# Two pairs of heads of every tile from 4 to 10 turned by way of DRAM, in a fused attention and mixture-of-experts kernel on one core

## Chip, core and metric

The kernel runs on one core of a Trainium2 chip, as one launch. The metric is the device time in microseconds (us) from the start to the end of a launch. Before the change the median of three runs is 717.74 us (717.74 to 717.99).

## What is computed

A banded attention feeds four weighted experts, whose output feeds a gated layer with a norm. All tensors are float32.

```python
def _attn_ref(q, k, v, n_global, n_local):          # 2 x 8 heads x 768 x 64, 8 global and 96 local keys
    ...
    scores = scale * np.matmul(q, k.transpose(0, 1, 3, 2))
    ...
    keep = is_global | is_local
    scores = scores + bias[None, :, :, :]           # a slope per head times the distance
    scores = np.where(keep, scores, -1000000000.0)
    a = np.exp(scores - np.max(scores, axis=-1, keepdims=True))
    a = a / (np.sum(a, axis=-1, keepdims=True) + 1e-09)
    return np.matmul(a, v).astype(np.float32)

def _moe_ref(x, domain_probs, w1, w2):              # 1536 tokens, 512 -> 1024 -> 512, 4 experts
    p = domain_probs / (domain_probs.sum(-1, keepdims=True) + 1e-09)
    for e in range(E):
        h = np.maximum(x @ w1[e], 0.0)
        out += p[:, e:e + 1] * (h @ w2[e])
    return out.astype(np.float32)

def _moe2_ref(x, w_in, w_out, g_ln):                # 512 -> 1024 -> 512
    h = x @ w_in
    e = np.exp(h - h_max)
    sm = e / (np.sum(e, axis=-1, keepdims=True) + 1e-09)
    solu = h * sm
    ln = (solu - mu) / np.sqrt(var + 1e-06) * g_ln
    return (ln @ w_out).astype(np.float32)
```

## The kernel before

The 1,536 tokens are 12 tiles of 128, and a tile's 8 heads are 4 pairs. A unit u is one pair of heads of one tile, tile u // 4 and pair u % 4, so there are 48 units. From unit 14 on the loop at lines 1578 to 1640 takes two units at a time: iteration t forms the scores of units t and t + 1, and brings earlier units further. The scheduler keeps the written order on each engine; an engine takes its instructions one after the other.

For a unit the steps are these. `scores` (L1224): TensorE forms sps, of which there is one buffer with room for two units, so the scores of t + 2 wait until VectorE has read those of t. `soft_pair` first sums and inverts the row sums of the units before (su, L1261 and L1262) and scales their probabilities p (L1266, on VectorE or GpSimd), then VectorE adds the bias and finds the row minimum (L1275, a custom instruction for each head, four per iteration), and ScalarE takes the exponential (L1282). Then p must be transposed, as TensorE needs the keys on the partitions. `stage_b` does it on TensorE (tile pt, L1306) and ScalarE copies the result out (pts, L1308). For the first two pairs of the tiles in `TURNED` the way is another: `turn` has VectorE transpose 32 x 32 blocks (L1324) and writes them to DRAM (t_dram, L1326), and two iterations later `turned_back` reads them into the one tile pts_turned with four transfers that put the blocks in place (L1331). In both ways `stage_c` multiplies by the values (x, L1357); a tile that is complete is rounded to xh on ScalarE (L1370) and its remainder xl is formed on VectorE (L1371), which is the input of the experts.

Between these steps TensorE is filled with products of the experts. They come from one generator in a fixed order, expert half 0 over the token blocks of 256, 256, 512 and 512 columns. `pull(share)` takes products until their cost has used up the credit, where `share` grows by what the iteration has not to do itself (`other`). A block can begin only when `tokens[0]` has reached its end: the third block needs 1,024 tokens, tiles 0 to 7. `tokens[0]` is set from `done` in the second half of an iteration. In a block's first GEMM (L553, from xh and xl) the fourth group's result fhh is made on VectorE (L565) and its remainder fhl too (L568); the second GEMM (L584) reads both, and VectorE weights its result into scr (L589).

GpSimd scales p, copies the overlap of the key tiles (L95) and, from t = 36 (`FORMS`), forms sums of xh and xl (L801) that begin with tiles 0 to 7. SyncE's queue issues every transfer of this stretch: values v (L1198), the write to t_dram, keys kr (L93), queries q (L1193) and the four reads.

```python
other = 870 * (not turned(t - 2)) + 550 * len(valued(t)) + 1100 * turned(t - 8)
share = 2 * (EARLY if t < N0 + 27 else LATE) + (1970 - other) // 2
```

Of the kernel before, what the change touches and what calls it, by code (L numbers as in the profile page):

```python
# [44 lines left out]
LOAD_AFTER = {2: [4], 3: [5], 4: [6], 5: [7], 6: [8, 9], 7: [10], 8: [11]}  # L45
SHARE = {11: 1000}
HALF = 512
PAIRS = 14
FORMS = 36
TURNED = 4, 6, 8, 9, 10  # L50
# [4 lines left out]
def kernel(ctx, tc, ep, qk, vp, nn, pr, wall, w64, gl, out):  # L55
# [1093 lines left out]
    def fast_arm():  # L1149
        st = stream("f")  # L1150
        with ExitStack() as es:
# [104 lines left out]
            def soft_pair(t):  # L1256

                if PAIRS < t <= NU:
                    st_rs.pop(t - 2), st_rs.pop(t - 1)
                    su = ss.tile([128, 4], F32, tag="su2", name="su2")  # L1260
                    nc.vector.tensor_reduce(out=su, in_=sums[:, (t // 2 - 1) % 3], op=ALU.add, axis=AX.X)  # L1261
                    nc.vector.reciprocal(out=su, in_=su)  # L1262
                    for u in (t - 2, t - 1):
                        p = st_p[u]
                        e = nc.gpsimd if turned(u) or t < NU and (u % 2 or t > FORMS) else nc.vector
                        e.tensor_tensor(out=p, in0=p, in1=su[:, 2 * (u % 2):2 * (u % 2) + 2].unsqueeze(2)  # L1266
                                        .to_broadcast([128, 2, 256]), op=ALU.mult)
# [43 lines left out]
            def turned(u):  # L1311

                return u % 4 < 2 and u // 4 in TURNED

            def valued(t):

                if turned(t - 4) or turned(t - 8) and t <= NU:
                    return []
                return list(range(t - 6 if turned(t - 10) and not turned(t - 6) else t - 4, t - 2))

            def turn(u0):
# [4 lines left out]
                nc.sync.dma_start(out=t_dram[u0 // 4 % 2], in_=blocks)  # L1326

            def turned_back(u0):
                t = pts_turned
                for jj in range(4):  # L1330
                    nc.sync.dma_start(out=t[32 * jj:32 * jj + 32].rearrange("r (i c) -> r i c", i=4),  # L1331
                                      in_=t_dram[u0 // 4 % 2].rearrange("(i r) (j c) -> j r i c", r=32, j=4)[jj])
# [4 lines left out]
            def stage_c(u, hold=None):  # L1337
# [23 lines left out]
                elif u >= N0 and pr_ == (1 if turned(u) else 3) and not turned(u - 2):  # L1361
# [216 lines left out]
            for t in range(PAIRS, NU + 3, 2):  # L1578

                other = 870 * (not turned(t - 2)) + 550 * len(valued(t)) + 1100 * turned(t - 8)  # L1580
# [6 lines left out]
                if turned(t - 8) and t <= NU:  # L1587
# [7 lines left out]
                if turned(t - 8):  # L1595
# [15 lines left out]
                for _ in range(2):  # L1611
                    next(rest_p, None)
                if t <= NU and not turned(t - 2):
# [12 lines left out]
                if t > NU and turned(t - 6):  # L1626
                    pull(share)
                    for u in (t - 6, t - 5):
                        stage_c(u)
# [3 lines left out]
                elif turned(t - 8):  # L1633
# [191 lines left out]
```

## Time and profile before

| | us |
|---|---|
| median of three runs (lowest, highest) | 717.74 (717.74, 717.99) |
| the profiled execution, its own time | 718.38 |
| its span in the trace | 716.6 |
| TensorE busy in it | 706.1 |
| VectorE, ScalarE, GpSimd busy | 497.8, 302.1, 349.2 |

The profile is of one execution. Its span is the time from the first to the last instruction, 1.8 us less than the execution's time. A line of a timeline gives the start in the span, the duration, the engine, the line of the kernel, what is written from what, how often in a row, and, in brackets, idle time before it with what ended it. Matmuls overlap, so what one costs is read from the start of one to the start of the next.

### The profile page before, as it was taken

What the parts mean: (1) busy time and instruction counts of PE and PEld (TensorE: products, weight loads), DVE (VectorE), ACT (ScalarE), POOL (GpSimd) and SP (SyncE); (2) the same over time, 40 slices, a digit from 0 to 9 for tenths busy, and PEclk for the clock granted to TensorE, in tenths of its full rate; (3) what the DMA queues carried; (4) which work ended last, traced back from release to release, by engine and by line L of the source; (5) the groups of instructions that cost most, each with busy time, mean ns of one, the idle gap of its engine ahead of it and who ended that gap; (6) DMA issues with size and microseconds to landing.
All of it is one profiled execution on the core that took longest, in us unless ns stands there. A gap on an engine that the chain in (4) does not pass through costs nothing.

```text
span 716.6 us, 11078 instructions
## 1 busy us (share of the span) xinstructions
PE 706.1 (99%) x3823; PEld 587.7 (82%) x3823; DVE 497.8 (69%) x1086; ACT 302.1 (42%) x678; POOL 349.2 (49%) x407
## 2 busy tenths in 40 slices
PE   7999999999999999999999999999999999999997
PEld 5688778888888889888888988888898888888886
DVE  6777665648776675776668578857964677777870
ACT  5877655432423333242243334324334324454442
POOL 6733475674883074227307323630745189455500
PEclk9999999999999999999999999999999999999999
DMA  8656762321351323233133323323322680424331
GB/s 251 153 162 167 181 172 88 102 74 45 111 164 49 118 91 101 82 95 118 45 117 113 95 73 118 118 77 100 103 89 74 267 349 1 137 101 138 106 124 49
DMA packets 59201, 84.56 MB, mean 118 GB/s; under 512 B 6144, under 2 KB 36608, under 8 KB 59136
## 3 DMA queue, kind: packets, MB, share of 16 engines
q1 hardware_dynamic: 58576, 83.34, 37.0%
q8 instruction: 32, 0.52, 0.3%
q10 hardware_dynamic: 560, 0.43, 0.2%
q14 instruction: 33, 0.27, 0.1%
HBM read 62.22 MB, written 21.52 MB: 117 GB/s over the span
## 4 chain that ended last, share of the span: by engine, by line
PE 95%; DVE 1%; ACT 1%; SPq 1%; DMA 1%; issue 0%; POOL 0%; DVEq 0%
PE fg L584 37%; PE fg L761 19%; PE fo L1089 9%; PE fh L990 8%; PE fg L676 7%; PE fg L553 6%; PE x L1357 3%; PE sps L1224 2%; PE pt L1306 2%; PE g L1384 1%; PE wp L135 1%; DMA pts_turned<-t_dram 1%; DVE fg L689 1%; ACT fhh L645 1%; PE fh L1070 0%
## 5 line engine op out<-in xcount | busy, mean ns | idle before, releaser
L584 PE MATMUL fg<-fhh,wV 128*128 128x512 f32 (+1 forms) x800 | 242.3, 384 | 0.4
L584 PEld LDWEIGHTS fg<-fhh,wV 128*128 128x128 f32 x800 | 148.0, 188 | 32.7 <-issue 2.7
L584 PE MATMUL fg<-fhl,wV 128*128 128x512 f32 (+1 forms) x400 | 149.1, 381 | 0.1
L584 PEld LDWEIGHTS fg<-fhl,wV 128*128 128x128 f32 x400 | 74.9, 188 | 14.9 <-DVE fhl L568 0.4
L310 POOL TENSOR_TENSOR wR<-kr,wR 128x512 fp32r<-128x512 f32 (+1 forms) x28 | 29.0, 1057 | 96.5 <-ACT wR L302 96.3
L645 ACT ACTIVATE fhh<-fg 128x512 fp32r<-128x512 f32 x80 | 47.5, 598 | 66.6 <-DVE fg L771 40.3
L603 POOL TENSOR_TENSOR scr<-scr,kr 128x512 f32<-128x512 f32 x24 | 31.0, 1292 | 61.4 <-DVE kr L602 61.4
L646 DVE SCALAR_TENSOR_TENSOR fhl<-fg,fhh 128x512 fp32r<-128x512 f32 x80 | 54.1, 687 | 6.9 <-ACT fhh L645 5.4
L761 PE MATMUL fg<-xt,fwS 128*128 128x512 f32 x252 | 58.3, 389 | 0.0
L761 PEld LDWEIGHTS fg<-xt,fwS 128*128 128x128 f32 x252 | 47.3, 188 | 9.8
L761 PE MATMUL fg<-xh,wR 128*128 128x512 f32 x168 | 54.0, 389 | 0.0
L771 DVE TENSOR_TENSOR fg<-kr,fg 128x512 f32<-128x512 f32 x42 | 29.1, 694 | 33.4 <-PE fg L761 22.9
L598 DVE TENSOR_TENSOR fg<-fg,pb 128x512 f32<-128x512 f32 x59 | 40.9, 693 | 15.1 <-PE fg L584 14.8
L1266 POOL TENSOR_TENSOR p<-p,su 128x512 f32<-128x512 f32 x24 | 27.9, 1178 | 38.7 <-ACT pts L1308 17.6
L1282 ACT ACTIVATE p<-p,mn 128x256 f32<-128x256 f32 x68 | 33.8, 499 | 23.3 <-DVE mn L1275 23.2
L599 DVE TENSOR_TENSOR scr<-fg,scr 128x512 f32<-128x512 f32 x59 | 40.8, 692 | 2.0
L553 PE MATMUL fg<-xh,wR 128*128 128x512 f32 (+1 forms) x128 | 38.9, 373 | 0.0
L761 PEld LDWEIGHTS fg<-xh,wR 128*128 128x128 f32 x168 | 31.5, 188 | 6.5
L310 POOL TENSOR_TENSOR fwS<-kr,fwS 128x512 fp32r<-128x512 f32 x28 | 35.7, 1296 | 1.6 <-ACT fwS L302 1.6
L1089 PE MATMUL fo<-xt,fhh 128*128 128x512 f32 (+1 forms) x156 | 35.4, 375 | 0.0
L766 ACT COPY kr<-fg 128x512 f32<-128x512 f32 x42 | 24.2, 590 | 25.6 <-PE fg L761 25.6
L1275 DVE CUSTOM_DVE_ANT_0 p<-sps,btab 128x256 f32<-128x256 f32 x68 | 25.0, 420 | 14.2 <-PE sps L1224 14.2
(286 smaller groups left out, 1503.3 us busy)
## 6 DMA issues: line engine op xcount, KB each, us to landing
w_dram<-fr SPq DMA_DIRECT2D x44, 256.0 KB, 2.4
kr<-in_wall_dram SPq DMA_DIRECT2D x42, 256.0 KB, 2.8
fr<-in_w_dram SPq DMA_DIRECT2D x32, 256.0 KB, 2.7
pb<-p_dram SPq DMA_DIRECT2D x22, 256.0 KB, 3.5
v<-in_vp_dram SPq DMA_DIRECT2D x10, 512.0 KB, 4.4
kr<-t_dram SPq DMA_DIRECT2D x32, 128.0 KB, 2.9
frawt<-in_wall_dram SPq DMA_DIRECT2D x14, 256.0 KB, 2.7
xt<-w_dram SPq DMA_DIRECT2D x6, 512.0 KB, 10.2
```

The lines of the kernel that those rows point to most:

```text
L310: e.tensor_tensor(out=w[:, 1], in0=t, in1=w[:, 0].bitcast(F32), op=ALU.subtract)
L553: nc.tensor.matmul(ps[:, :n], lhsT=w[:, a, k], rhs=b[:, k, cols], start=(k == 0 and i == 0), stop=(k == 3 and i == 2))
L584: nc.tensor.matmul(ps[:, :n], lhsT=w[:, a, k], rhs=b[k], start=(i == 0), stop=(i == 11))
L598: nc.vector.tensor_tensor(out=ps[:, :n], in0=ps[:, :n], in1=pg, op=ALU.mult)
L599: nc.vector.tensor_tensor(out=a, in0=ps[:, :n], in1=a, op=ALU.add)
L645: nc.scalar.activation(th, src, AF.Relu)
L646: residuals.append(lambda: nc.vector.scalar_tensor_tensor(out=tl, in0=src, scalar=0.0, in1=th.bitcast(F32), op0=ALU.max, op1=ALU.subtract))
L676: nc.tensor.matmul(ps[:, q_ * q:q_ * q + q_], lhsT=w[:, a, j], rhs=x[b][j], start=(opens and q == j == m == 0), stop=(j == 1 and m == 2), ...
L761: nc.tensor.matmul(ps, lhsT=w[:, a, j], rhs=x[b][j], start=(i in (1, 2, 5) and j == 0 and m == 0), stop=(j == 1 and m == 2), skip_group_ch ...
L990: nc.tensor.matmul(ps[i], lhsT=left[i][x][j], rhs=right[i][j][:, y], start=(i in (1, 5, 2) and j == m == 0), stop=(j == 1 and m == 2), ski ...
L1089: nc.tensor.matmul(ps, lhsT=a[:, fc % 4], rhs=wo[fc][:, i % 2, c0:c0 + n], start=(fc == i == 0), stop=(fc == 7 and i == 2))
L1282: nc.scalar.activation(p[:, a], p[:, a], AF.Exp, bias=mn[:, a:a + 1], scale=-1.0, accum_out=st_rs[u][:, a, 0:1])
```

## The change

Two pairs of heads, units 4s and 4s + 1, of each tile s from 4 to 10 are turned through DRAM; before, tiles 5 and 7 were transposed by TensorE. `ended(t)` says that t is the iteration in which a tile's turned units of t - 8 are valued. `BOTH`, empty here, would name tiles whose other two pairs are turned as well, and the code for it adds nothing as long as it is empty. The place in t_dram was by tile, `u0 // 4 % 2`, and is by pair now, `u0 // 2 % 2`, which is 0 for all units that are turned. The table `LOAD_AFTER` brings the keys of one tile per tile. Unit 15 is scaled on VectorE instead of GpSimd.

```diff
--- before.py
+++ after.py
@@ -42,12 +42,13 @@
 
 RING = 4
 KEY_OF = [0, NI] + list(range(1, NI)) + list(range(NI + 1, 2 * NI))
-LOAD_AFTER = {2: [4], 3: [5], 4: [6], 5: [7], 6: [8, 9], 7: [10], 8: [11]}
+LOAD_AFTER = {2: [4], 3: [5], 4: [6], 5: [7], 6: [8], 7: [9], 8: [10], 9: [11]}
 SHARE = {11: 1000}
 HALF = 512
 PAIRS = 14
 FORMS = 36
-TURNED = 4, 6, 8, 9, 10
+TURNED = 4, 5, 6, 7, 8, 9, 10
+BOTH = ()
 LATE = 680
 
 
@@ -1262,7 +1263,7 @@
                     nc.vector.reciprocal(out=su, in_=su)
                     for u in (t - 2, t - 1):
                         p = st_p[u]
-                        e = nc.gpsimd if turned(u) or t < NU and (u % 2 or t > FORMS) else nc.vector
+                        e = nc.gpsimd if turned(u) or t < NU and (u % 2 and t > PAIRS + 2 or t > FORMS) else nc.vector
                         e.tensor_tensor(out=p, in0=p, in1=su[:, 2 * (u % 2):2 * (u % 2) + 2].unsqueeze(2)
                                         .to_broadcast([128, 2, 256]), op=ALU.mult)
                 for u in (t, t + 1) if t < NU else ():
@@ -1310,26 +1311,30 @@
 
             def turned(u):
 
-                return u % 4 < 2 and u // 4 in TURNED
+                return u // 4 in (TURNED if u % 4 < 2 else BOTH)
 
             def valued(t):
 
-                if turned(t - 4) or turned(t - 8) and t <= NU:
+                if turned(t - 4) or ended(t) and t <= NU:
                     return []
-                return list(range(t - 6 if turned(t - 10) and not turned(t - 6) else t - 4, t - 2))
+                return list(range(t - 6 if t % 4 == 2 and turned(t - 10) and not turned(t - 6) else t - 4, t - 2))
+
+            def ended(t):
+
+                return t % 4 == 0 and turned(t - 8)
 
             def turn(u0):
                 for u in (u0, u0 + 1):
                     p, k = st_p.pop(u), 4 * (u % 2)
                     nc.vector.transpose(out=blocks.rearrange("p (jj c q) -> p c jj q", jj=4, c=8)[:, k:k + 4],
                                         in_=p.rearrange("p a (c jj f) -> p (a c) jj f", c=2, jj=4))
-                nc.sync.dma_start(out=t_dram[u0 // 4 % 2], in_=blocks)
+                nc.sync.dma_start(out=t_dram[u0 // 2 % 2], in_=blocks)
 
             def turned_back(u0):
-                t = pts_turned
+                t = pts_all[:, 2:4].rearrange("p u c q -> p (u c q)") if u0 % 4 else pts_turned
                 for jj in range(4):
                     nc.sync.dma_start(out=t[32 * jj:32 * jj + 32].rearrange("r (i c) -> r i c", i=4),
-                                      in_=t_dram[u0 // 4 % 2].rearrange("(i r) (j c) -> j r i c", r=32, j=4)[jj])
+                                      in_=t_dram[u0 // 2 % 2].rearrange("(i r) (j c) -> j r i c", r=32, j=4)[jj])
                 t = t.rearrange("p (i c q) -> p c i q", i=4, c=8)
                 for u in (u0, u0 + 1):
                     st_pt[u] = [t[:, 4 * (u % 2) + c] for c in range(4)]
@@ -1358,7 +1363,7 @@
                                          start=(c == 0), stop=(c == nch - 1))
                 if u < N0 and s == NAT - 1:
                     xc = slice(pr_, pr_ + 1), slice(0, 128 * NAT)
-                elif u >= N0 and pr_ == (1 if turned(u) else 3) and not turned(u - 2):
+                elif u >= N0 and pr_ == (1 if s in TURNED and s not in BOTH else 3):
                     xc = slice(0, 4), slice(128 * s, 128 * s + 128)
                 else:
                     return
@@ -1577,14 +1582,14 @@
                     st.load_piece()
             for t in range(PAIRS, NU + 3, 2):
 
-                other = 870 * (not turned(t - 2)) + 550 * len(valued(t)) + 1100 * turned(t - 8)
+                other = 870 * (not turned(t - 2)) + 550 * len(valued(t)) + 1100 * ended(t) * (1 + turned(t - 6))
                 share = 2 * (EARLY if t < N0 + 27 else LATE) + (1970 - other) // 2
                 hold, landed = [], copies[:]
                 del copies[:]
                 if t < NU:
                     for u in (t, t + 1):
                         scores(u)
-                if turned(t - 8) and t <= NU:
+                if ended(t):
                     for u in (t - 8, t - 7):
                         stage_c(u, hold)
                 if t < NU:
@@ -1592,7 +1597,7 @@
                         next_operands(*divmod(u, 4))
                 if turned(t - 4):
                     turned_back(t - 4)
-                if turned(t - 8):
+                if ended(t):
                     load_v((t - 8) // 4 + 2)
                 soft_pair(t)
                 for f in landed:
@@ -1610,6 +1615,9 @@
                     pull(share)
                 for _ in range(2):
                     next(rest_p, None)
+                if ended(t) and turned(t - 6):
+                    for u in (t - 6, t - 5):
+                        stage_c(u)
                 if t <= NU and not turned(t - 2):
                     for u in (t - 2, t - 1):
                         stage_b(u)
@@ -1623,14 +1631,10 @@
                 for u in valued(t):
                     if u in st_pt:
                         stage_c(u)
-                if t > NU and turned(t - 6):
-                    pull(share)
-                    for u in (t - 6, t - 5):
-                        stage_c(u)
                 if t % 4 == 2 and not turned(t - 6):
                     done = (t - 2) // 4
                     load_v(done + 1)
-                elif turned(t - 8):
+                elif ended(t):
                     done = (t - 4) // 4
                 if t == FORMS:
                     st.forms = st.x_forms(lambda: [st.rawp.tile([128, 512], F32, tag="raw", name="fraw")
```

On TensorE, iterations t = 34 and 36 before (a scores instruction in four parts opens each; fg is an expert's product, pt a transpose, x the values):

```order
L1224 MATMUL sps<-kr,q 128x256 x4
L584 MATMUL fg<-fhh,wV 128x256
L584 MATMUL fg<-fhl,wV 128x256
L584 MATMUL fg<-fhh,wV 128x256 x2
L584 MATMUL fg<-fhl,wV 128x256
L584 MATMUL fg<-fhh,wV 128x256
L1357 MATMUL x<-pts,v 64x128 x16
L1224 MATMUL sps<-kr,q 128x256 x4
L1306 MATMUL pt<-ident,p 128x128 x8
L553 MATMUL fg<-xh,wR 128x512
L553 MATMUL fg<-xl,wR 128x512
L553 MATMUL fg<-xh,wR 128x512 x2
L553 MATMUL fg<-xl,wR 128x512
```

The same engine now, from the scores of t = 32 to those of t = 38 and the first product behind them:

```order
L1225 MATMUL sps<-kr,q 128x256 x4
L1362 MATMUL x<-pts_turned,v 64x128 x8
L1307 MATMUL pt<-ident,p 128x128 x8
L1225 MATMUL sps<-kr,q 128x256 x4
L1362 MATMUL x<-pts,v 64x128 x8
L1225 MATMUL sps<-kr,q 128x256 x4
L1362 MATMUL x<-pts_turned,v 64x128 x8
L1307 MATMUL pt<-ident,p 128x128 x8
L1225 MATMUL sps<-kr,q 128x256 x4
L554 MATMUL fg<-xh,wR 128x512
```

The products of t = 32, 34 and 36 have moved to earlier iterations (up to t = 30) and to later ones, so scores, turned values, transposes and values follow each other.

On VectorE, from the second custom of t = 28 to the first weighting, before (the ISA rows are the customs and their minima):

```order
L1275 ISA mn 128x1
L1371 TENSOR_TENSOR xl<-x,xh 128x4x128
L1275 ISA p,mn<-sps,btab 128x256
L1275 ISA mn 128x1
L1275 ISA p,mn<-sps,btab 128x256
L1275 ISA mn 128x1
L565 TENSOR_SCALAR fhh<-fg 128x256
L568 SCALAR_TENSOR_TENSOR fhl<-fg,fhh 128x256
L589 TENSOR_TENSOR scr<-fg,pb 128x256
```

The same work now stands at t = 26, behind the turn of units 24 and 25 (tmp_170 is the block buffer):

```order
L1276 ISA p,mn<-sps,btab 128x256
L1276 ISA mn 128x1
L1329 STREAM_TRANSPOSE tmp_170<-p 128x4x4x32 x2
L566 TENSOR_SCALAR fhh<-fg 128x256
L569 SCALAR_TENSOR_TENSOR fhl<-fg,fhh 128x256
L590 TENSOR_TENSOR scr<-fg,pb 128x256
L1262 TENSOR_REDUCE su_1017<-sums 128x4
L1263 RECIPROCAL su_1017<-su_1017 128x4
```

The fourth group's fhh and fhl and the first weighting have moved from behind the customs of t = 28 to right behind the turn of t = 26.

On SyncE, from the write of t = 26 to the next reads, before:

```order
L1326 DMA t_dram<-tmp_170 128x1024
L1198 DMA v<-in_vp_dram 128x1024
L93 DMA kr<-in_qk_dram 64x4x128 x4
L1193 DMA q<-in_qk_dram 64x4x128 x2
L1331 DMA pts_turned<-t_dram 32x4x256 x4
L93 DMA kr<-in_qk_dram 64x4x128 x2
L1193 DMA q<-in_qk_dram 64x4x128 x2
```

Now:

```order
L1331 DMA t_dram<-tmp_170 128x1024
L94 DMA kr<-in_qk_dram 64x4x128 x2
L1194 DMA q<-in_qk_dram 64x4x128 x2
L1336 DMA pts_turned<-t_dram 32x4x256 x4
L1199 DMA v<-in_vp_dram 128x1024
L1331 DMA t_dram<-tmp_170 128x1024
```

The values v stand behind the reads, two key transfers instead of four ahead of them, and a turn's transfers stand in every second iteration.

## Rows read from the trace of the kernel before

**Rows 1.** The page, busy time of the engines and the chain that ended last.
```profile
PE 706.1 (99%) x3823; PEld 587.7 (82%) x3823; DVE 497.8 (69%) x1086; ACT 302.1 (42%) x678; POOL 349.2 (49%) x407
...
PE 95%; DVE 1%; ACT 1%; SPq 1%; DMA 1%; issue 0%; POOL 0%; DVEq 0%
```

**Rows 2.** The waits of TensorE from 40 to 250 us: total, times, longest.
```profile
PE x L1357 <- DMA pts_turned<-t_dram: 0.5, 1, 0.5
PE pt L1306 <- DVE p L1266: 0.3, 1, 0.3
PE pt L1306 <- POOL p L1266: 0.2, 1, 0.2
```

**Rows 3.** Timeline of TensorE from 43 to 61 us, t = 18 to 26.
```profile
43.48 0.39 PE L584 MATMUL fg<-fhh,wV 128*128 128x256 f32 x1
...
46.17 1.09 PE L1357 MATMUL x<-pts,v 128*64 128x128 f32 x16
...
52.88 0.39 PE L553 MATMUL fg<-xh,wR 128*128 128x256 f32 x1
...
53.70 1.03 PE L1306 MATMUL pt<-ident,p 128*128 128x128 f32 x8
54.49 0.36 PE L553 MATMUL fg<-xh,wR 128*128 128x256 f32 x1
...
55.38 1.09 PE L1357 MATMUL x<-pts,v 128*64 128x128 f32 x16
...
60.98 1.13 PE L1224 MATMUL sps<-kr,q 64*128 64x256 f32 x8
```

**Rows 4.** Timeline of TensorE at t = 28, from 67 to 70 us.
```profile
67.80 1.03 PE L1306 MATMUL pt<-ident,p 128*128 128x128 f32 x8
...
69.33 0.39 PE L584 MATMUL fg<-fhl,wV 128*128 128x256 f32 x1
```

**Rows 5.** Timeline of VectorE: the turn of t = 26, fhh of t = 28.
```profile
63.88 1.29 DVE L1324 STREAM_TRANSPOSE tmp<-p 128x512 f32<-128x512 f32 x2
...
68.40 0.42 DVE L565 TENSOR_SCALAR fhh<-fg 128x256 fp32r<-128x256 f32 x1
```

**Rows 6.** Timeline of GpSimd: scalings of t = 26, first sums at t = 36.
```profile
61.83 2.04 POOL L1266 TENSOR_TENSOR p<-p,su 128x512 f32<-128x512 f32 x2 [4.24 <-PE sps L1224]
...
86.78 1.29 POOL L801 TENSOR_TENSOR fraw<-xh,xl 128x512 f32<-128x512 f32 x1 [0.47 <-DVE xl L1371]
```

**Rows 7.** Timeline of TensorE at t = 32, scores and turned values.
```profile
75.06 1.14 PE L1224 MATMUL sps<-kr,q 64*128 64x256 f32 x8
76.70 1.09 PE L1357 MATMUL x<-pts_turned,v 128*64 128x128 f32 x16 [0.50 <-DMA pts_turned<-t_dram]
```

**Rows 8.** Timeline of VectorE from 76 to 85 us, t = 32 to 36.
```profile
76.25 0.42 DVE L1275 CUSTOM_DVE_ANT_0 p<-sps,btab 128x256 f32<-128x256 f32 x1 [0.87 <-PE sps L1224]
...
79.35 0.69 DVE L1371 TENSOR_TENSOR xl<-x,xh 128x512 fp32r<-128x512 f32 x1 [0.18 <-ACT xh L1370]
...
80.15 0.18 DVE L1262 RECIPROCAL su<-su 128x4 f32<-128x4 f32 x1
...
84.71 0.69 DVE L1266 TENSOR_TENSOR p<-p,su 128x512 f32<-128x512 f32 x1
```

**Rows 9.** Timeline of ScalarE at t = 32: xh, behind the exponentials.
```profile
78.76 0.56 ACT L1370 CAST xh<-x 128x512 fp32r<-128x512 f32 x1
```

**Rows 10.** SyncE's queue: the write of t = 26 and its reads.
```profile
65.20 0.34 SPq L1326 DMA_DIRECT2D t_dram<-tmp  x1
...
70.20 2.02 SPq L1331 DMA_DIRECT2D pts_turned<-t_dram  x4
```

**Rows 11.** The tile pts_turned: time from issue to landing.
```profile
DMA to landing us min/median/max: 2.5/4.3/5.5
```

**Rows 12.** Windows of core 0: busy time of engines, clock, DMA share.
```profile
0.00:20.00 20.00, 16.42 (x97) 10.72 (x97) 13.34 (x75) 11.13 (x44) 13.38 (x30) 1.00 0.83 249
...
710.00:716.60 6.60, 1.52 (x13) 1.32 (x11) 0.00 (x0) 0.47 (x1) 0.00 (x0) 0.77 0.16 50
```

## The prediction

> **What bounds the kernel now.** I read the page first: TensorE is busy 706.1 of 716.6 us and the chain of waits that ended last lies on it for 95% [rows 1]. So a change pays only if TensorE has less to do or waits less. The waits of TensorE from 40 to 250 us are three, 1.0 us together: for the DMA that brings turned probabilities back, and for two scalings of p [rows 2]. The changed stretch, iterations t = 14 to 48 of attention, has hardly anything to gain but TensorE's own work, and much that can be uncovered. Then I read the timelines of TensorE, VectorE, GpSimd and SyncE for t = 20 to 40.
>
> **What is removed.** Units 20, 21, 28 and 29 are no longer transposed by TensorE: two pairs of units, 16 transposes. At t = 22 such a pair starts at 53.70 and the next product at 54.49, so 0.79 us [rows 3]. It also cuts a run of MoE products in two. 21 products in one run take 2.69 us (43.48 to 46.17), 0.128 each; the 12 products around this pair take 52.88 to 55.38 less 0.79, 1.71, where one run would take 1.54. So 0.17 for a cut, and 0.96 for a pair: 1.9 for both. By the order of instructions the products of t = 20 to 48 stand in six runs fewer than before; two of the six are the pairs', four more at 0.17 give 0.7. Saved: **2.6 us**. ScalarE loses four copies of pts, GpSimd and VectorE exchange a few scalings; neither sets the pace there, so nothing.
>
> **What is moved: the fill.** The planner counts 870 ns less beside a turned pair, so it pulls more MoE products into t = 22 to 30. The first two blocks (256 columns) are then used up at t = 30, where before they last to t = 34. The third block needs 1,024 tokens, which stand ready once tile 7 is valued. Tile 7's end moves from t = 34 to t = 36, since its first pair now comes back through DRAM; block 3 starts at t = 38 instead of 36. So t = 32, 34 and 36 have no product at all. No product is lost: 18 of 512 columns just come after attention. This costs in three places.
>
> **Wait A, t = 26.** Before, the first products of the second GEMM stand at t = 28, behind scores and customs alone, and wait 0.6 us: the pair of transposes starts at 67.80, the second product after it at 69.33 where 68.71 would be due [rows 4]. Now nine of them come at t = 26 without waiting and the tenth needs fhh of ft 3, which VectorE makes behind the two transposes of units 24 and 25. Those wait for GpSimd's two scalings. Before, GpSimd ends them at 63.87 and VectorE turns from 63.88 for 1.29 us [rows 5, 6]. The turn that t = 22 gains puts up to 1.2 us ahead of this on VectorE, of which its idle time takes a part: I take 0.7 later. Turn done 65.3, fhh 0.4 on [rows 5], 65.7, fhl 66.0. TensorE starts these scores at 61.2 (60.98 before [rows 3], and 0.2 more as t = 22 now has 21 products and no pair), needs 1.07 for them and 12 x 0.128 for the products, and stands at 63.8. **2.2 us**; with no shift 1.5, with all of it 2.7.
>
> **Wait B, t = 32 to 38.** Without products an iteration is as long as the chain of softmax, as scores has one buffer. The steps show at t = 32 of before: scores start at 75.06, the first custom at 76.25, the four exponentials are done and xh starts at 78.76, xl at 79.35, the reciprocal of the sums ends at 80.33 [rows 7 to 9]. That is 5.27 from scores to sums, 2.51 from first custom to last exponential. Where scores(32) start follows from TensorE's own work: scores(26) at 61.2; t = 26 with 18 products, 2.3, wait A and a value of a pair, 1.0, brings scores(28) to 67.8; t = 28 with turned values, 1.0, and 12 products and a pair of transposes, 2.5, brings scores(30) to 72.4; t = 30 with 21 products, 2.7, and a value brings scores(32) to 77.1. From there the sums are ready at 82.4, the exponentials of t = 34 at 84.9, sums 0.6 later, a scaling on VectorE 0.65 [rows 8], four customs 1.4: 87.6, when scores(38) may start. TensorE's own work in between is three scores (3.2), two turned values (2.0), two pairs of transposes (1.6), one value of a pair (1.0), 7.9 of 10.5 us. So 2.6 idle. Then block 3's first product waits for xl of tile 7: exponentials of t = 36, xh 0.59, xl 0.61, at 89.85, while scores(38) end at 88.67: 1.2. **3.8 us**. Bounds: 2.6 if xl of tile 7 comes in time after all, 4.5 if transposes and values also wait for their scaling and copies in turn.
>
> **Wait C, t = 40 and 44.** From t = 36 on GpSimd has sums of x between its scalings, and they stand first in its queue. The first waits for xl of tile 7: before it starts at 86.78, and GpSimd then has two sums of 1.3 and two scalings of 2.04 by turns [rows 6]. From 89.85 two sums, p(36, 37), two sums end at 97.1, and p(38) and p(39) at 98.1 and 99.1. TensorE reaches their transposes at 96.7: from 89.85 nine products of 512 columns, each counted as two of 256 (0.24), a value, scores, turned values, and six more products. 1.4 for the one and 0.7 for the other, 2.1, and by the same count 0.7 at t = 44. That is **2.8 us**, within 0.5 (if TensorE comes later than I count) and 4.
>
> **The DRAM round trip.** A turn is now due every 4 steps, with one buffer (t_dram[0]) and one tile pts_turned; the next write waits until the last read-back has landed, the next read-back until the values of the pair before are formed. Its price: before, a write at 65.20, the first read at 70.20, and values at 76.70 that had waited for it, so 11.4 in all [rows 10, 7], with v and four key transfers ahead of the reads. Now v stands behind the reads and two key transfers are ahead; a single read lands after 2.5 to 5.5, median 4.3 [rows 11]. I take 8.6, within 7.5 and 11.4. By 8.6 the values of t = 36 come when TensorE is there, so nothing is added; at 9.8 waits of 2.0 and 2.6 at t = 36 and 40 take the place of C, and the sum grows by about 1. The Trainium skill (SBUF — State Buffer, The DMA setup-cost knee) fits a transfer as 2 us plus its bytes at 436 GB/s; for 512 KB each way that is an estimate of 3.2 + 3.2 = 6.4 us and would add nothing. The rows show nearly twice that, so I go by them.
>
> **Small parts.** Unit 15's scaling on VectorE is 0.69 [rows 8] at t = 16; no row shows TensorE waiting near it, and it delays customs by at most 0.7: 0, at worst 0.5. Keys one tile later: scores of tile 9 need them at t = 36, loaded from t = 32: more than 8 us against 3 to 5; 0. The eight reads and two writes more keep SyncE's queue waiting; behind them stand v and later keys, needed an iteration on: 0.
>
> **Sum.** New waits 2.2 + 3.8 + 2.8 = 8.8. Old waits that go: 1.0 [rows 2] and 0.6 [rows 4]. Saved work 2.6. 8.8 - 1.6 - 2.6 = **+4.6 us**. After attention TensorE has no idle time until the last microseconds, so nothing is given back. On the profiled execution (718.38 us, span 716.6) this is 723.0; it stood 0.64 above the median of the runs shown, so I forecast 717.74 + 4.6 = **722.3 us**. About 1.4 us (0.2%) can be told from no change.
>
> **Rivals.**
> 1. *The fill suffices (faster).* Place: TensorE at t = 26 and t = 32 to 36. If GpSimd and VectorE are done with p(24, 25) and fhh before TensorE has made the nine products, and the softmax chain of t = 32 to 36 keeps TensorE less than about 2 us idle, only the saved work counts: -2.6, with the old wait for DMA gone up to -3, 715 to 716. For it: TensorE is the bound, waits are 1.0 us. Against: three iterations with 2.1 to 2.9 us of TensorE's work each and a chain of 3.5 to 5.3. It decides at 4.2 us of new waits (2.6 + 1.6): below that, faster. Chance 0.11; that they cancel within 1.4 us, 0.07.
> 2. *The DRAM round trip sets the pace.* If write to landing stays at 10.8 or more, values at t = 28, 32, 36, 40, 44 each wait, as each round starts only when the one before has ended: 10.8 against iterations of about 9 us is 2 us a time, against A to C which it covers in part: +7 to +12, 725 to 730. For it: 11.4 in rows 10 and 7. Against: that had more ahead of it. Chance 0.16.
> 3. *Smaller waits.* B and C half as large: +1.5 to +3, 719.2 to 720.7. Chance 0.08.
> 4. *The clock falls.* In the stretch from 710 us TensorE is busy 1.52 of 6.6 and the granted clock is 0.77; in the first 20 us it is busy 16.42 and keeps 1.00 [rows 12]. Were t = 32 to 38, about 10 us with 7.9 of work, to run at the lower of the two levels (1.2 for 2.4 GHz), it would add up to 8: 730. The rows speak against it: with 3.6 us of idle time the first 20 us kept the clock, and no wait I count is as long as the idle time at the end. Chance 0.02. The Trainium skill (TensorE: Matmul & The Clock Gate, Part 1: The HAM clock gate) says that idle time puts the clock back to the lower level; the trace agrees at the end of the span and shows it nowhere else.
>
> **How the numbers follow.** My forecast, +3 to +7, 0.56; rivals 0.11, 0.07 (no change), 0.16, 0.08, 0.02. Faster 0.11, same 0.07, slower 0.82. The range leaves out faster and same (0.18) and the far end of rival 2: 719.2 to 728.5. The forecast's own range is 720.7 to 724.7.
>
> **What would show it.** Right: in TensorE's timeline a gap of about 2 before a product with fhh at t = 26, no product from t = 32 to 36, waits there for VectorE's customs, block 3 starting near 90, transposes at t = 40 waiting for GpSimd's p; 120 transposes; and 24 products of 512 left when attention ends. Wrong: pts_turned's DMA as the largest releaser (rival 2); TensorE's waits below 4 us (rival 1); a granted clock below 1.00 near 80 us (rival 4).

## The result and the profile after

| | before | changed |
|---|---|---|
| median, us | 717.84 (717.74 to 717.99, 4 runs) | 726.72 (726.0 to 727.6, 4 runs) |
| ratio to before | | 1.0124, 95% interval 1.0107 to 1.0142 |
| profiled execution, its span | 718.38, 716.6 | 726.07, 724.3 |
| TensorE busy | 706.1 | 705.7 |

The change costs 8.9 us by the medians and 7.7 by the two profiled executions. From the page of the changed kernel, busy time of the engines (compare [rows 1]; line numbers of the changed kernel are one to five higher than before):

```profile
PE 705.7 (97%) x3807; PEld 586.1 (81%) x3807; DVE 499.8 (69%) x1089; ACT 299.8 (41%) x674; POOL 349.8 (48%) x408
```

TensorE has 16 instructions and 0.4 us less, and still the span is 7.7 us longer: the time went into waiting. The waits of TensorE from 40 to 250 us (total, times, longest), to be held against [rows 2]:

```profile
PE fg L585 <- DVE fhh L566: 1.9, 1, 1.9
PE pt L1307 <- POOL p L1267: 1.9, 3, 1.2
PE fg L585 <- DVE xl L1376: 1.4, 1, 1.4
PE x L1362 <- DMA pts_turned<-t_dram: 1.1, 1, 1.1
PE x L1362 <- ACT pts L1309: 0.8, 1, 0.8
PE fg L762 <- DVE fg L772: 0.8, 1, 0.8
PE x L1362 <- PE pt L1307: 0.6, 1, 0.6
PE sps L1225 <- DVE mn L1276: 0.5, 1, 0.5
PE fg L554 <- DVE xl L1376: 0.2, 1, 0.2
```

Three kinds of wait have become nine. Their places, in the timeline of TensorE of the changed kernel:

```profile
63.56 0.28 PE L585 MATMUL fg<-fhh,wV 128*128 128x256 f32 x1
65.72 0.38 PE L585 MATMUL fg<-fhh,wV 128*128 128x256 f32 x1 [1.89 <-DVE fhh L566]
66.18 0.39 PE L585 MATMUL fg<-fhl,wV 128*128 128x256 f32 x1
...
77.34 1.13 PE L1225 MATMUL sps<-kr,q 64*128 64x256 f32 x8
...
82.42 1.09 PE L1362 MATMUL x<-pts,v 128*64 128x128 f32 x16 [0.83 <-ACT pts L1309]
...
86.45 1.09 PE L1362 MATMUL x<-pts_turned,v 128*64 128x128 f32 x16 [1.13 <-DMA pts_turned<-t_dram]
...
88.50 1.13 PE L1225 MATMUL sps<-kr,q 64*128 64x256 f32 x8
...
90.30 0.50 PE L554 MATMUL fg<-xl,wR 128*128 128x512 f32 x1 [0.22 <-DVE xl L1376]
...
98.52 0.66 PE L1307 MATMUL pt<-ident,p 128*128 128x128 f32 x4 [1.19 <-POOL p L1267]
99.52 0.66 PE L1307 MATMUL pt<-ident,p 128*128 128x128 f32 x4 [0.34 <-POOL p L1267]
...
125.35 1.97 PE L1362 MATMUL x<-pts,v 128*64 128x128 f32 x32 [0.55 <-PE pt L1307]
128.72 0.50 PE L585 MATMUL fg<-fhh,wV 128*128 128x512 f32 x1 [1.40 <-DVE xl L1376]
...
134.41 0.39 PE L554 MATMUL fg<-xh,wR 128*128 128x512 f32 x1
```

Read it downwards. At 63.56 the ninth product of the second GEMM starts at t = 26, and the tenth comes at 65.72 instead of 63.68: wait A. From 77.34 to 88.50 four scores follow each other with no product between, and values wait for copies, scores for VectorE, values for the read-back: wait B, which ends when the second product of block 3 gets its xl at 90.30. At 98.52 and 99.52 transposes wait for GpSimd's scalings: wait C. The lines at 125.35 and 128.72 are of no step of the prediction. At 134.41 block 4 starts. In the kernel before the same product starts at 127.07, so 7.3 of the 7.7 us are lost by then; three lines of TensorE there:

```profile
123.69 1.97 PE L1357 MATMUL x<-pts,v 128*64 128x128 f32 x32
125.59 0.50 PE L584 MATMUL fg<-fhh,wV 128*128 128x512 f32 x1
...
127.07 0.50 PE L553 MATMUL fg<-xh,wR 128*128 128x512 f32 x1
```

The first of these are the last values of attention. The second line continues a group of products that was begun inside attention, and follows the values without a wait. On VectorE of the changed kernel stand the two events of A, and two that explain the end of attention:

```profile
64.65 0.71 DVE L1329 STREAM_TRANSPOSE tmp<-p 128x512 f32<-128x512 f32 x1 [0.26 <-POOL p L1267]
65.28 0.39 DVE L566 TENSOR_SCALAR fhh<-fg 128x256 fp32r<-128x256 f32 x1
...
124.56 0.68 DVE L1376 TENSOR_TENSOR xl<-x,xh 128x512 fp32r<-128x512 f32 x1
127.97 0.69 DVE L1376 TENSOR_TENSOR xl<-x,xh 128x512 fp32r<-128x512 f32 x1 [2.72 <-ACT xh L1375]
```

The second transpose ends, fhh is made at 65.28, and TensorE's tenth product starts at 65.72, as it ends: A waits for VectorE, where fhh stands behind the transposes. The first value of tile 11 (125.35) needs the one buffer of x, which xl of tile 10 (124.56 to 125.24) has to read first; the profile names the transposes as what ended that wait, so this too is concluded from the times. The first product behind attention (128.72) starts when xl of tile 11 (127.97) is done. It begins a new group, and behind attention groups come from a new pool of PSUM banks (L907). That its bank has to wait until x is read is concluded from these two times; the run on the end of attention, below, puts it to the test.

GpSimd for wait C (compare [rows 6], where the first sum starts at 86.78):

```profile
90.32 1.29 POOL L802 TENSOR_TENSOR fraw<-xh,xl 128x512 f32<-128x512 f32 x1 [2.89 <-DVE su L1262]
...
97.42 2.04 POOL L1267 TENSOR_TENSOR p<-p,su 128x512 f32<-128x512 f32 x2
```

The first sum starts 3.5 us later than before, the scalings of units 38 and 39 run from 97.42 to 99.46, and the transposes follow each of them.

SyncE's queue for the wait at 86.45, the write whose values are formed there:

```profile
76.62 0.34 SPq L1331 DMA_DIRECT2D t_dram<-tmp  x1
```

From this write to its values it takes 9.8 us.

### The profile page after: what moved, and what is told of

It is laid out like the page before. It is cut to its first block, busy times and chain, and to the rows that moved or that the text cites. A ratio compares the mean times of both kernels' runs of the same rounds, so it can differ in the third digit from the quotient of the medians.

```text
span 724.3 us, 11073 instructions
## 1 busy us (share of the span) xinstructions
PE 705.7 (97%) x3807; PEld 586.1 (81%) x3807; DVE 499.8 (69%) x1089; ACT 299.8 (41%) x674; POOL 349.8 (48%) x408
## 4 chain that ended last, share of the span: by engine, by line
PE 92%; DVE 2%; POOL 2%; ACT 1%; issue 1%; DMA 1%; SPq 0%; DVEq 0%; POOLq 0%
PE fg L585 36%; PE fg L762 18%; PE fo L1090 9%; PE fh L991 8%; PE fg L677 7%; PE fg L554 5%; PE x L1362 3%; PE sps L1225 2%; PE pt L1307 2%; POOL p L1267 1%; PE g L1389 1%; PE wp L136 1%; DMA pts_turned<-t_dram 1%; DVE fg L690 1%; POOL fraw L802 1%
## 5 line engine op out<-in xcount | busy, mean ns | idle before, releaser
L762 PE MATMUL fg<-xl,wR 128*128 128x512 f32 x84 | 32.7, 389 | 0.0
```

The costliest lines, as they stand in the source:

```text
L762: nc.tensor.matmul(ps, lhsT=w[:, a, j], rhs=x[b][j], start=(i in (1, 2, 5) and j == 0 and m == 0), stop=(j == 1 and m == 2), skip_group_ch ...
```

## Experiments

Each is a change to the changed kernel, unless it says otherwise. Ratios are to the kernel before, measured beside it.

**The small parts alone** (keys one tile at a time, unit 15 on VectorE, one DRAM buffer):

```diff
-TURNED = 4, 5, 6, 7, 8, 9, 10
+TURNED = 4, 6, 8, 9, 10
```

> The changed kernel with tiles 4, 6, 8, 9 and 10 turned, as before: only the keys one tile at a time, unit 15 on VectorE and the one DRAM buffer are left of the change. TensorE's order is that of the kernel before. Theory (three waits of TensorE and a fourth at the end of attention, all made by turning tiles 5 and 7): 717.8 us, within 0.7 of before. Rival (one DRAM buffer or the late keys cost by themselves): 719 or more, with a new wait for pts_turned or kr.

717.45 us, ratio 0.9989 (0.9980 to 0.9998). They cost nothing and may bring a little: the wait for the read-back at t = 32 is 0.2 us instead of the 0.5 of [rows 7]. So the loss is of tiles 5 and 7. Which of the three parts brings it wasn't tried.

**Tile 5 alone:**

```diff
-TURNED = 4, 5, 6, 7, 8, 9, 10
+TURNED = 4, 5, 6, 8, 9, 10
```

> Tile 5 turned too, tile 7 not. Theory: wait A stays (1.9 us for fhh at t = 26, plus 0.2 for fhl), waits B, C and that at the end of attention go, as tile 7 ends at t = 34 again and 6 products are left at the end as before; one pair of transposes saved. 717.8 + 2.1 - 0.6 - 1.0 - (0 to 0.5) = 718.3 us, 717.5 to 719. Rival (the DRAM round trip sets the pace): waits for pts_turned at t = 28 and 32, 720 or more.

721.09 us, ratio 1.0033 (1.0020 to 1.0046): by the ratios 3.2 us above the small parts alone, where 0.5 was expected (718.3 against 717.8). A is there, 1.9 us, and no wait for the read-back. The rest shows in the timeline of TensorE behind it:

```profile
66.78 1.53 PE L1362 MATMUL x<-pts,v 128*64 128x128 f32 x16
68.25 2.08 PE L1225 MATMUL sps<-kr,q 64*128 64x256 f32 x8
70.25 1.29 PE L1362 MATMUL x<-pts_turned,v 128*64 128x128 f32 x16
71.47 0.39 PE L585 MATMUL fg<-fhh,wV 128*128 128x256 f32 x1
```

The values take 1.47 us to the next start, the scores 2.00, the turned values 1.22, where they take 1.02, 1.07 and 1.02 otherwise: 1.6 us more for the same instructions. The windows of this run (columns: stretch, us, busy time and count of TensorE, its weight loads, VectorE, ScalarE and GpSimd, then granted clock, DMA share, GB/s):

```profile
60.00:65.50 5.50, 3.65 (x29) 2.92 (x27) 4.27 (x15) 3.92 (x14) 2.27 (x3) 1.00 0.83 199
65.50:71.40 5.90, 5.79 (x46) 4.21 (x46) 2.81 (x10) 0.50 (x2) 1.45 (x1) 0.71 0.81 257
```

The granted clock is 1.00 before the gap and 0.71 in the stretch behind it (0.50, the lower level of 1.2 GHz, from 68 to 70 us). This is rival 4, to which the prediction gave 0.02, at another place. Another 0.9 us are at t = 36, whose transposes wait 1.2 us for VectorE's scaling instead of 0.3 [rows 2].

**Tile 7 alone:**

```diff
-TURNED = 4, 5, 6, 7, 8, 9, 10
+TURNED = 4, 6, 7, 8, 9, 10
```

> Tile 7 turned too, tile 5 not. Theory: wait A goes, the waits of t = 34 to 40 (B and C) and the wait of 1.4 us for the first product behind attention stay: changed kernel 726.7 less 1.3 to 2 for A and plus 1.0 for the pair of transposes that comes back: 725.5 us, 724 to 727. Rival (tile 5's turn is what costs): under 721.

724.07 us, ratio 1.0088 (1.0073 to 1.0103). By the ratios that is 7.1 us above the small parts alone, where tile 5 is 3.2: tile 7 is the larger part. It takes the fill away, moves the tokens of block 3 and leaves 24 products at the end. The 1.4 us behind attention are there to the hundredth. Here the read-back is waited for, 1.7 us at t = 36, and behind that gap the granted clock is 0.52 from 84.9 to 88.2 us.

**A, undone by VectorE's order alone.** The turn of t = 26 is written behind the first pull:

```diff
-                if turned(t - 2):
+                if turned(t - 2) and t != 26:
                     turn(t - 2)
...
                     pull(share)
+                if t == 26:
+                    turn(t - 2)
```

> The changed kernel with the turn of t = 26 written behind the first pull, so that VectorE makes fhh and fhl before the two transposes. Theory (wait A is VectorE's order): TensorE waits under 0.5 us for fhh instead of 1.9, scores(28) start 2 us earlier and the rest follows: 726.7 - 2 = 724.7 us, 723.5 to 725.5; the spread of runs with a lower mean clock goes down too if the idle time at t = 26 was what lowered it. Rival (the softmax chain of t = 32 to 38 takes it up, or the later turn comes back too late for t = 32): 726 or more, with a new wait for pts_turned.

725.22 us, ratio 1.0096 (1.0083 to 1.0109): 6.8 us above before by the medians, where the changed kernel is 8.9, so 2.1 less; the intervals just touch, so the trace has to show where it comes from. On VectorE fhh now stands first:

```profile
63.66 0.42 DVE L566 TENSOR_SCALAR fhh<-fg 128x256 fp32r<-128x256 f32 x1
...
64.45 1.30 DVE L1329 STREAM_TRANSPOSE tmp<-p 128x512 f32<-128x512 f32 x2
```

TensorE's waits for fhh and for the read-back in this run:

```profile
PE x L1362 <- DMA pts_turned<-t_dram: 2.2, 1, 2.2
...
PE fg L585 <- DVE fhh L566: 0.3, 1, 0.3
```

A is down from 1.9 to 0.3, and scores(28) start at 66.40 instead of 68.00, so A is VectorE's order. But this is not yet what the kernel gains. At t = 36 the read-back is waited for 2.2 us instead of 1.1, and the granted clock is 0.50 from 88 to 90 us. Two lines, of TensorE and of GpSimd:

```profile
91.04 0.39 PE L554 MATMUL fg<-xl,wR 128*128 128x512 f32 x1
```

```profile
88.72 1.26 POOL L802 TENSOR_TENSOR fraw<-xh,xl 128x512 f32<-128x512 f32 x1 [2.88 <-DVE su L1262]
```

The product that needs xl starts at 91.04, 0.7 us later than in the changed kernel: on TensorE the whole gain of A is used up there. GpSimd has kept it. Its first sum starts at 88.72 instead of 90.32, so the transposes of t = 40 no longer wait for it (0.3 us in all, at t = 44, instead of 1.9), and block 4 starts 1.6 us sooner (132.84 against 134.41). Of that, 0.8 is lost again at 192 us, where the wait for VectorE is 1.5 us instead of 0.8. The mean granted clock of its five runs is 0.996 to 0.998, no higher than the changed kernel's 0.998 to 1.000: the narrower spread that was expected of taking A's gap away did not come.

**C, undone by GpSimd's order alone:**

```diff
-                if t == FORMS:
+                if t == FORMS + 2:
```

> The changed kernel with GpSimd's sums of x begun at the end of t = 38 instead of 36, so that the scalings of units 36 to 39 stand ahead of them. Theory (wait C is GpSimd's order): the waits of 1.2 and 0.3 us at t = 40 go, 726.7 - 1.5 = 725.2 us, 724.3 to 726. Rival (what waits there is late for another reason, the softmax chain or the copies): no change, 726 to 727.5, the transposes of t = 40 waiting as long.

725.64 us, ratio 1.0110 (1.0094 to 1.0125). The intervals overlap, so the time alone doesn't tell it from the changed kernel; the trace does. The wait for GpSimd at t = 40 is gone (0.2 us at t = 36 is new), and t = 40 takes from 94.40 to 101.05, 6.65 us, instead of 93.37 to 102.18, 8.81. So C is GpSimd's order. Of these 2.2 us, 0.6 are given back behind attention: block 4's second GEMM takes 11.6 us instead of 11.0, with a wait for fhl. The profile of this run also has a lower clock behind A, which the changed kernel's has not.

**The end of attention.** Six products more in t = 48, so that what is left begins in the middle of a group:

```diff
-                    pull(share)
+                    pull(share + 1280 * (t == NU))
```

> The changed kernel with six more products in the last iteration (t = 48), so that 18 are left behind attention, the first six of a group that is begun. Theory (a new group behind attention must wait until xl of the last tile has been formed, and half a group covers that): the waits of 1.4 and 0.6 us go, 726.7 - 1.9 = 724.8 us, 724 to 725.6. Rival (that wait belongs to the work left, and only moves): 726 to 727.5, with the same wait elsewhere.

724.70 us, ratio 1.0091 (1.0076 to 1.0106): 6.3 us above before instead of 8.9, so 2.6 less, where 1.9 was expected. Both waits are gone from TensorE's list, and the products follow the last values as they do before. In this profile scores(38) start 1.0 us later than in the changed kernel, as the clock fell behind A, and block 4 starts 0.9 us sooner (133.48), so 2.0 us are gained between the two, as much as the two waits. Only the place at which attention stops was changed: t = 48 has six products in the changed kernel, nine before and twelve here. More products there give xl of tile 10 its time, and half a group behind the last values gives it to xl of tile 11.

**DRAM, first in the changed kernel, then without starving.** Two places in t_dram by turns:

```diff
-                nc.sync.dma_start(out=t_dram[u0 // 2 % 2], in_=blocks)
+                nc.sync.dma_start(out=t_dram[u0 // 4 % 2], in_=blocks)
...
-                                      in_=t_dram[u0 // 2 % 2].rearrange("(i r) (j c) -> j r i c", r=32, j=4)[jj])
+                                      in_=t_dram[u0 // 4 % 2].rearrange("(i r) (j c) -> j r i c", r=32, j=4)[jj])
```

> The changed kernel with the tiles' places in t_dram by turns, so that a write need not wait for the read-back of the tile before. Theory (the changed kernel waits for DMA once, 1.1 us at t = 36; A, B, C and the end do not hang on DRAM): 726.7 less 0 to 1.1: 726.2 us, 725 to 727. Rival (the DRAM round trip sets the pace of the changed kernel): under 723.

727.53 us, ratio 1.0134 (1.0118 to 1.0149). The wait for the read-back is gone from TensorE's list, and nothing is gained: the transposes of t = 36 wait for VectorE and GpSimd instead (0.4 and 0.2 us). Wait B is as long without the read-back as with it: from scores(32) to the product that needs xl it takes 12.94 us (78.46 to 91.40), in the changed kernel 12.96. This run's order on TensorE is that of the changed kernel, which makes it a second look at the clock:

```profile
60.67 1.13 PE L1225 MATMUL sps<-kr,q 64*128 64x256 f32 x8
...
69.01 1.23 PE L1225 MATMUL sps<-kr,q 64*128 64x256 f32 x8
...
78.46 1.13 PE L1225 MATMUL sps<-kr,q 64*128 64x256 f32 x8
...
91.40 0.50 PE L554 MATMUL fg<-xl,wR 128*128 128x512 f32 x1 [0.22 <-DVE xl L1376]
```

```profile
65.30:69.00 3.70, 3.62 (x22) 2.87 (x22) 1.77 (x5) 0.00 (x0) 1.45 (x1) 0.57 0.88 265
```

From scores(26) to scores(28) it takes 8.34 us, with a granted clock of 0.57 behind the gap; the changed kernel's profile has 6.91 (61.09 to 68.00) at 1.00. Same instructions, same gap of 1.9 us, 1.4 us apart. The Trainium skill (TensorE: Matmul & The Clock Gate, Part 1: The HAM clock gate) says that the number of matmuls at the lower clock at the start of a kernel differs between runs of one kernel; these two profiles show such a difference in the middle of one.

Then the fill. The planner counts 870 ns in every iteration, so products are left for t = 32 to 36, and 30 at the end:

```diff
-                other = 870 * (not turned(t - 2)) + 550 * len(valued(t)) + 1100 * ended(t) * (1 + turned(t - 6))
+                other = 870 + 550 * len(valued(t)) + 1100 * ended(t) * (1 + turned(t - 6))
```

> The changed kernel, but the planner counts 870 ns in every iteration, turned or not, so that products are left for t = 32, 34 and 36, and 30 are left at the end instead of 24. Theory (starving is what costs): fhh comes two iterations later, wait A goes (-2.1), the idle time before t = 38 goes down from 2.5 to under 1, the wait behind attention goes as half a group is left (-1.4), the wait for GpSimd at t = 40 stays: 726.7 - 2 - 2 - 1.4 = 721 us, 718 to 723. Rival (the DRAM round trip sets the pace): the waits turn into waits for pts_turned at t = 32, 36 and 40, and it stays above 724.

722.35 us, ratio 1.0049 (1.0033 to 1.0064): 4.0 us above before, so 4.9 of the loss are gone, with A, B and the wait behind attention. The largest wait that is left is rival 2's; besides, TensorE waits 1.0 us for GpSimd. TensorE's wait for the read-back, and SyncE's writes to t_dram:

```profile
PE x L1362 <- DMA pts_turned<-t_dram: 3.9, 5, 1.5
```

```profile
66.24 0.34 SPq L1331 DMA_DIRECT2D t_dram<-tmp  x1
...
75.02 0.34 SPq L1331 DMA_DIRECT2D t_dram<-tmp  x1
...
84.66 0.34 SPq L1331 DMA_DIRECT2D t_dram<-tmp  x1
...
93.75 0.34 SPq L1331 DMA_DIRECT2D t_dram<-tmp  x1
```

Each write from 66.24 on starts within 0.1 us of the start of the values for which TensorE had waited, so when the read-back before it has landed. Round for round that is 8.8, 9.6 and 9.1 us. I had taken 8.6 in the prediction; the estimate by the Trainium skill's fit (SBUF — State Buffer, The DMA setup-cost knee), 6.4, is too short here. Keys and queries go between write and read; how much of the difference is theirs was not tried.

With both, even fill and two places:

> The even fill of the run before with the two places in t_dram. There the waits for pts_turned were 3.9 us in five places, each write starting just when the read-back of the tile before had landed. Theory (once TensorE doesn't starve, the round trip of 8.8 to 9.6 us through one buffer is the bound, and the second buffer takes the wait of the write away): 722.35 - 3 = 719.3 us, 718 to 720.5, with waits for pts_turned under 1 us. Rival (the one tile pts_turned or the transfers' own time is the bound): no gain, above 721.5.

720.55 us, ratio 1.0039 (1.0026 to 1.0051). Waits for the read-back are down from 3.9 to 1.6 us, but 1.8 were gained by the medians where 3 were expected, and the intervals overlap: transposes come earlier and wait for GpSimd, 1.7 us instead of 1.0, and two read-backs are still late (0.9 us the longer).

**All waits at once.** Even fill, two places in t_dram, sums begun at t = 38, and tiles 5, 7 and 9 read back into the half of pts_all that turned units leave unused:

```diff
-                t = pts_all[:, 2:4].rearrange("p u c q -> p (u c q)") if u0 % 4 else pts_turned
+                t = pts_all[:, 0:2].rearrange("p u c q -> p (u c q)") if u0 // 4 % 2 else pts_turned
```

> Both pairs of every tile from 4 to 10 turned as in the changed kernel, with even fill, two places in t_dram, the sums of x begun at t = 38, and tiles 5, 7 and 9 read back into two unused places of pts, so that a read-back need not wait for the values of the tile before. Theory (all waits that the change made come from order and from single buffers): against the run with even fill and two places, 720.55, less 1.1 for GpSimd at t = 40 and 1.6 for the read-backs: 717.8 us, 716.8 to 719, so level with the kernel before or up to 1.5 us faster. Rival (the transfers themselves are too slow): no gain on 720.55, with waits for pts or pts_turned over 1 us.

718.55 us, ratio 1.0002 (0.9990 to 1.0015): level with before. So order, fill and single buffers together account for the whole loss, and turning two more pairs is worth nothing measurable with these means. Not every wait is gone: TensorE waits 2.2 us from 40 to 250 us, where before it is 1.0. Part of the saved work also goes behind attention, as the timeline of TensorE shows (the first products of block 4, of its second GEMM and of what follows):

```profile
126.46 0.40 PE L554 MATMUL fg<-xh,wR 128*128 128x512 f32 x1
...
137.39 0.39 PE L585 MATMUL fg<-fhh,wV 128*128 128x512 f32 x1
...
149.01 0.39 PE L554 MATMUL fg<-xh,wR 128*128 128x512 f32 x1
```

Block 4 starts at 126.46, 0.6 us sooner than before. Its second GEMM then takes 11.6 us instead of 10.9, and a wait of 0.6 us for VectorE follows at 185 us.

The sums were then caught up at t = 46, against this run:

```diff
-                    for f in st.forms.pop(0):
+                    for f in st.forms.pop(0) + (st.forms.pop(0) if t == NU - 2 else []):
```

> The run with all waits taken out, where the sums of x that begin later are caught up at t = 46. There 0.7 us were lost behind attention: the second of its GEMMs took 11.6 us where it takes 10.9 otherwise, with a wait for fhl. Theory (that loss comes from sums and their rounding left over for behind attention): 718.55 - 0.7 = 717.9 us, 717 to 718.6, level with the kernel before or slightly faster. Rival (the loss is of another cause, or the sums now hold up unit 46 and 47): 718.5 or more.

719.18 us, ratio 1.0005 (0.9991 to 1.0020). That GEMM is back at 11.0 us, but attention ends 0.9 us later: the transposes of units 46 and 47 wait 0.5 us for VectorE, and a read-back at t = 24, ahead of the edit and so not made by it, is waited for 0.4 us longer. Nothing is gained.

**Tile 5 with the same means** (even fill, two places, two tiles for the read-back):

> Only tile 5 turned in addition, with even fill, two places in t_dram and two tiles for the read-back. Theory (one pair of transposes saved, no starving and no late tokens as tile 7 stays on TensorE): the kernel with the small parts alone, 717.45, less 1.0 for the pair: 716.5 us, 715.5 to 717.5, faster than before by 0.1 to 0.4%. Rival (even fill pulls too little ahead of t = 36 and tiles 8 to 10 wait as before): 718 or more.

719.60 us, ratio 1.0023 (1.0013 to 1.0032): a miss. Attention ends 1.2 us sooner than with the small parts alone (first product behind it at 123.95 against 125.19), but 18 products are left instead of 6, and transposes wait 1.7 us for GpSimd in four places. It may be that even fill pulls too little where tile 7 gives no reason to save; that was not tried further.

## Why the prediction was right, and where it fell short

- **The bound and the sign** held: TensorE does less and waits more. A, B and C stand where they were put. The size did not hold: +8.9 was measured for +4.6, and 726.7 lies above the forecast's own 720.7 to 724.7. It lies inside the full range only because that takes in rival 2's 725 to 730, and rival 2 is not what happened; that the time fell inside it is luck.
- **A** was 2.2; measured 2.0 for fhh (63.68 to 65.72) and 0.3 for fhl, 2.4. The run with the turn behind fhh shows that it is VectorE's order. The end of the turn at 65.3 was right (64.65 and 0.71 give 65.36), but not by the working as it is written: 63.88, 0.7 later and 1.29 for the turn would be 65.9. Only the second transpose had to wait for GpSimd; the first starts at 63.68.
- **B** was 3.8. From scores(32) to the product that waits for xl it takes 12.96 us (77.34 to 90.30), of which TensorE's own work is four scores, two turned values, two pairs of transposes, one value and one product, 9.15: 3.8. The profile marks 2.7 of it as waits; the rest is longer steps from start to start, such as 1.03 instead of 0.79 for a pair of transposes ahead of scores. The parts were not those of the prediction. Scores wait only 0.5 for VectorE, and 1.1 is the read-back, which it had put at nothing. That the length came out all the same is no accident: with two places in t_dram that wait is gone and B is as long, so VectorE, GpSimd and ScalarE end just as late.
- **C** was 2.8. At t = 40 1.35 us from the end of the products to 98.52 and 0.6 between the two halves; at t = 44 0.9: 2.9.
- **Saved work** was 2.6, of it 0.96 for a pair. From scores(22) to scores(24) the changed kernel takes 4.80 us with nine products more than before and no pair, before 4.59; nine products are 1.07, so a pair is 0.86, and 2.4 in all if the 0.7 for the other cuts is right, which was not measured.
- **The sum** ended with "After attention TensorE has no idle time until the last microseconds, so nothing is given back." That is the step that failed. It was read from the kernel before, where half a group covers xl of the last tile. The change moves the place at which attention stops to the start of a group, and 0.6 and 1.4 us come up that no row of before shows. With them, 4.6 becomes 6.6 of the 7.3 us at the start of block 4, and with the terms as measured here 7.1.
- **Behind that** the changed kernel waits 0.8 us for VectorE at 192 us, which itself waits for a write to w_dram to land. That write is waited for 1.1 us before and 2.4 now. Runs with tile 5 or 7 alone don't have the wait of TensorE. What makes the write land later was not tried, and stays open.
- **The clock** (rival 4, 0.02) was thought to need longer idle time than any of these waits. Six of the profiles of the twelve runs show the granted clock at 0.50 to 0.56, about the lower level, in a stretch of 2 us behind a gap of 1.7 to 2.2 us: tile 5 alone, tile 7 alone, the turn behind fhh, the later sums, the six products more and the two places. It costs about 1.5 us each time, by the same instructions' starts at 1.00; the changed kernel's profile doesn't show it. That the four runs of the changed kernel lie 1.4 us apart (726.0 and 726.1, 727.4 and 727.6) agrees with it in size: the mean granted clock is 1.000 in the first two and 0.998 in the others. It doesn't show it, as the kernel before has 0.998 to 1.000 too in the 17 runs beside the first experiments, and its times do not follow the clock. Where the clock fell in the runs at 727 isn't recorded.
- **Rival 2** (DRAM) was rightly not the bound: the second buffer alone gains nothing. But its price was too low: 8.6 was taken, and the changed kernel takes 9.8 from the write at 76.62 to the values at 86.45 (before, the two rows give 11.5 and not 11.4). At 9.8 the prediction expected waits of 2.0 and 2.6 in place of C; there is one of 1.1, inside B. With even fill the read-back became the largest wait.

## What to carry to other kernels

When a change takes work from the bounding engine, ask first what the planner does with the credit: here 18 products moved out of the iterations that needed cover, and each term of the loss was a wait that they had covered. Read the cover at the boundary of a stage as well as inside it; where the filling stops in a group decides whether a new pool of buffers must be waited for. And with several bounds close behind each other, undo all of them before judging an idea: one at a time gave 0 to 4.9 us, all together 8.4, and only that showed how little was left to win with these means.

## What was not expected of the hardware

In six profiles a gap of 1.7 to 2.2 us on TensorE was followed by a granted clock of about 0.5 within the next 4 us. In four of them it is the gap of A, with TensorE busy before and after; in the other two (tile 7 alone, the turn behind fhh) it is the read-back at t = 36, with shorter waits ahead of it. With tile 5 alone that made values and scores 1.6 us longer, so the echo of the wait cost nearly as much as the wait of 1.9 us. In the run with even fill five waits, 3.9 us together, left the clock at 1.00, and so did the gap of 1.9 us in the changed kernel's own profile.
